# Two edits to the transfers of a fused attention and two-layer network kernel: the queue of the outputs, and the program place of the next phase's weight loads

## The chip, the cores and the metric

The kernel runs on one core of a Trainium2 chip. A core has five engines that run side by side, each through its own list of instructions in order: TensorE (PE: matrix products, with the weight loads in PEld), VectorE (DVE), ScalarE (ACT), GpSimd (POOL) and SyncE (SP), which here only issues transfers. A transfer (DMA) is issued by an instruction in an engine's list, waits there for its semaphores, and then runs on 16 DMA engines that all queues share. The metric is the device time of one execution in microseconds (us); the median of several runs counts. Before the change it is 1300.45 us (three runs: 1300.34, 1300.45, 1306.09).

## The reference

```python
def _attn_ref(q, k, v, tau):            # 4 batches, 8 heads, 576 rows, 64 wide
    scores = (1 / sqrt(64)) * q @ k.T
    scores = where(scores >= max(scores) - tau, scores, -1e9)
    attn = exp(scores - max(scores));  attn /= sum(attn) + 1e-9
    return attn @ v
x = attn_out as (2304, 512)              # 4 x 576 tokens
h = x @ w_in;  g = (a0 + a1*h + a2*h^2 + a3*h^3) / (1 + |b0|*|h| + |b1|*h^2 + 1e-6)
x = g @ w_out                            # w_in 512 x 2048, w_out 2048 x 512
h = x @ w2_in;  g = h if h >= 1, 0 if h <= -1, else (h + 1)^2 / 4
return g @ w2_out                        # (2304, 512) float32
```

## The kernel before

Each batch passes through three stages: attention, the first network (MoE1, `m == 0`) and the second (MoE2, `m == 1`). The networks run in eight phases, MoE1 and MoE2 of batch 0, then of batch 1, and so on (L664). A phase has 24 steps (L665): three blocks `j` of 192 tokens, and in each block the eight chunks `i` of the inner width of 2048. A step makes the first product (L645, into `ph`), a nonlinear function on ACT and DVE, a split into two float16 parts (`gg`, ACT L191 and POOL L195), and, three steps later (`LAG`), the second product (L659, into `acc`). Attention of batches 1 to 3 is cut into units that are laid beside the steps of the networks of the batch before (`ATTENTION`, L32): batch 1 beside steps 18 to 50, batch 2 beside 60 to 100, batch 3 beside 108 to 147.

The weights of one network, in float16 parts, fill eight tiles `wc` of 1 MB, one per chunk. Both networks share these eight places, so at each of the seven changes of phase the next phase's chunk `i` is loaded from scratch memory into the place of chunk `i` (`load_chunk`, L259) once the last block's second product has used it. L703 and L704 do this at the end of `finish_step`, in the last block, directly after that second product has been written into the program. The load waits for TensorE's last matmul on the place; that wait follows from the tile pool, whatever the place in the program.

At the end of a block of MoE2, `end_moe2` (L613) scales `acc` (ACT L615), turns it by TensorE (L621), copies each of two pieces out of PSUM by ACT (L623, tile `ot`) and issues a transfer of the piece to the output (L629): 24 transfers in all, of 128 or 256 KB.

All transfers are issued from SP's list: inputs (L310, L313), the transposes by DMA of attention's probabilities (L384, `eT` from `hl`, 144 of them, one per row block), those of q and k (L333), chunk loads (L261) and outputs (L629). An `eT` transpose waits for POOL's last piece of `hl` (L382) and is waited for by TensorE's product with v (L397). A later transfer in SP's list is not issued while an earlier one waits.

The order in each engine's list isn't written out by hand: the framework's scheduler sets it with a modelled time line, by readiness and by priorities given through `at(step)`, L158. Transfers take one of eight completion semaphores in turn, and one waits until the former transfer on its semaphore has landed.

Of the kernel before, what the change touches and what calls it, by code (L numbers as in the profile page):

```python
# [36 lines left out]
def tile_attention_moe_moe2(  # L37
# [18 lines left out]
    V, A, G, T, Q = nc.vector, nc.scalar, nc.gpsimd, nc.tensor, nc.sync  # L56
# [8 lines left out]
    NCH = 8  # L65
# [190 lines left out]
    def new_chunk(m, i):  # L256
        return wp.tile([P, 2 * HALF], F16, name=f"wc{m}_{i}", tag="wc")

    def load_chunk(m, i):  # L259
        wc = new_chunk(m, i)  # L260
        Q.dma_start(wc, scratch[m][i])  # L261
        return wc
# [334 lines left out]
    def flat(t):  # L597
        return t.rearrange("p (z d) t -> p z d t", z=2)
# [14 lines left out]
    def end_moe2(b, j, acc, consts):  # L613
        o = mp.tile([P, KT, TB], F32, name=f"o{b}_{j}", tag="yo", bufs=1)
        A.activation(flat(o), acc[:, :, 0 : 2 * TB].rearrange("p z (d t) -> p z d t", d=2), AF.Copy, scale=consts[4])  # L615
        cuts = sorted({j * TB, (j + 1) * TB} | {t * P for t in range(NT + 1) if j * TB < t * P < (j + 1) * TB})
        for c0, c1 in zip(cuts, cuts[1:]):
            n, t, p0 = c1 - c0, c0 // P, c0 % P
            pt = ps_1.tile([P, DM], F32, name=f"pt{b}_{j}_{c0}", tag="aux")
            for d in range(KT):  # L620
                T.transpose(pt[0:n, d * P : (d + 1) * P], o[:, d, c0 - j * TB : c1 - j * TB], ident)  # L621
            ot = mp.tile([P, DM], F32, name=f"ot{b}_{j}_{c0}", tag="wt", bufs=N_WT)
            A.copy(ot[0:n], pt[0:n])  # L623
            dst = out[b * S : (b + 1) * S, :]
            if t < NT:
                dst = dst[0 : NT * P, :].rearrange("(p t) d -> t p d", t=NT)[t, p0 : p0 + n, :]
            else:
                dst = dst[c0:c1, :]
            Q.dma_start(dst, ot[0:n])  # L629

    chunks = {}

# [20 lines left out]
    def second_product(m, i, gg, acc):  # L653
        w = chunks[m, i][:, HALF:].rearrange("p (x f d) -> p x f d", x=2, f=NF)
        for f in range(NF):
            for d in range(KT):
                dst = acc[:, d // 2, (d % 2) * TB : (d % 2 + 1) * TB]
                for n, (wx, gx) in enumerate(((0, 0), (0, 1), (1, 0))):
                    T.matmul(dst, w[:, wx, f, d * P : (d + 1) * P], gg[:, gx, f, :],  # L659
                             start=(i == 0 and f == 0 and n == 0 and d % 2 == 0),  # L660
                             stop=(i == NCH - 1 and f == NF - 1 and n == 2), skip_group_check=True)
# [9 lines left out]
    for n in range(N_UNITS):  # L671
        with at(2 * n - 40):
            next(att)
        while halves and len(halves) * N_UNITS > 2 * NCH * (N_UNITS - 1 - n):
            with at(2.4 * (2 * NCH - len(halves)) - 40):
                i, x = halves.pop(0)
# [11 lines left out]
        spread(first, last, [("att", b)] * N_UNITS)  # L688
    spread(*WEIGHTS, [("w", i, x) for i in range(NCH) for x in range(2)])

    pending, consts, accs, atts = [], {}, {}, {}

    def finish_step():
        n, m, b, j, i, gg, _ = pending.pop(0)
        if i == 0:
            accs[m, b, j] = ps_2.tile([P, 1024], F32, name=f"acc{m}_{b}_{j}", tag="acc").rearrange("p (z n) -> p z n", z=2)
        acc = accs[m, b, j]
        behind = pending[-1][-1] if n > 0 and len(pending) == LAG else None
        with tc.issue_after(behind) if behind is not None else nullcontext():
            second_product(m, i, gg, acc)  # L700
        if i == NCH - 1:
            (end_moe1 if m == 0 else end_moe2)(b, j, acc, consts[m, b, j])
        if j == NB - 1 and n + 1 < len(phases) and phases[n + 1][0] != m:  # L703
            chunks[1 - m, i] = load_chunk(1 - m, i)  # L704

    for st, (n, m, b, j, i) in enumerate(steps):
        with at(st):
            if i == 0:
                if m == 0:
                    consts[m, b, j] = moe1_consts(b) if j == 0 else consts[m, b, 0]  # L710
                else:
                    if b == 0 and j == 0:
                        moe2_weights()
                    consts[m, b, j] = moe2_consts(b, j)
            gg, last = first_product(m, b, j, i, consts[m, b, j])
        pending.append((n, m, b, j, i, gg, last))
        if len(pending) > LAG:
            with at(st + 1.5):
                finish_step()
        for t, u in beside[st]:  # L720
            if u[0] == "w":
                with at(t - 3):
                    stage_half(1, u[1], u[2], False)
            else:
                if u[1] not in atts:
                    atts[u[1]] = attention(u[1])
                with at(t - 1.5):
                    next(atts[u[1]])
    while pending:
        with at(st + 1.5):  # L730
            finish_step()
# [28 lines left out]
```

## Time and profile before

| | |
|---|---|
| median of three runs | 1300.45 us |
| profiled execution, device time | 1302.72 us |
| its span, first to last instruction | 1300.9 us |
| busy: PE, DVE, ACT, POOL | 1053.0, 1018.2, 841.7, 569.0 us |
| mean granted clock of TensorE | 0.925 of full speed |
| SP's transfers: packets' time on the 16 engines | 56.2% of the span |

A stretch of the span stands as start:end in us. In the rows, `SPq` is SP's issuing list, and `SPq L629 <- ACT ot L623` is time in which SP stood at a transfer of L629 until ACT had done L623. A duration of an issue is the time that SP spent issuing; the landing of the data comes later. `x2` merges two like instructions, with the time from the start of the first to the end of the last. Busy time of a stretch counts each engine apart, and a group's share over the whole run mixes stages with different limits, so the rows below are mostly of single stretches.

### The profile page before, as it was taken

Reading aid. Unit: us, or ns where it says so; the run is one execution under the profiler, and the core shown is the slowest. Engines: PE = TensorE matmul, PEld = TensorE weight load, DVE = VectorE, ACT = ScalarE, POOL = GpSimd, SP = SyncE. Lnnn points to the kernel's source line nnn. Section 1 sums busy time; section 2 is a strip of 40 time slices with the busy share of each in tenths; the row PEclk is TensorE's granted clock in tenths of the full one; section 3 lists DMA queues with packets and bytes.
Section 4 is the critical chain, followed back from the end, with each engine's and each line's share of the span. In section 5 each row is a group of like instructions: output and inputs, shape, how many; then the busy total and the mean of one; then the engine's idle time right before and its main releaser. Section 6 shows DMA issues by size and latency. Waiting matters only on the chain.

```text
span 1300.9 us, 31793 instructions
## 1 busy us (share of the span) xinstructions
PE 1053.0 (81%) x12498; PEld 959.5 (74%) x12498; DVE 1018.2 (78%) x2461; ACT 841.7 (65%) x1515; POOL 569.0 (44%) x781
## 2 busy tenths in 40 slices
PE   1465445687745888899889999999799999999998
PEld 1243324687744787789878898898688898999997
DVE  6667777899959887679999676889998677897431
ACT  4767655776745666667776576777765667776332
POOL 3858665454433545431146365422354554122221
PEclk9996656888966999999999999999989999999999
DMA  7878896323577667881279376911765669106100
GB/s 220 222 172 218 233 230 195 129 101 112 196 276 208 120 111 122 184 217 40 62 189 231 71 130 137 246 30 42 192 176 122 102 105 266 47 2 209 52 14 26
DMA packets 260277, 187.14 MB, mean 144 GB/s; under 512 B 220960, under 2 KB 233248, under 8 KB 251936
## 3 DMA queue, kind: packets, MB, share of 16 engines
q1 hardware_dynamic: 260128, 185.12, 56.2%
q8 instruction: 98, 1.61, 0.5%
q14 instruction: 51, 0.42, 0.1%
HBM read 106.96 MB, written 21.50 MB: 99 GB/s over the span
## 4 chain that ended last, share of the span: by engine, by line
PE 30%; DVE 26%; DMA 13%; issue 10%; POOL 10%; ACT 6%; SPq 2%; DVEq 0%; POOLq 0%; ACTq 0%
PE acc L659 13%; PE ph L645 13%; DMA eT<-hl 8%; POOL hl L382 5%; DVE e L371 2%; DMA qkT<-qk 2%; POOL wc L195 2%; PE pv L397 2%; DVE t L532 2%; DVE t L537 2%; DVE t L538 2%; DMA rqk<-in_k_dram 2%; DVE t L539 1%; DVE wt L212 1%; DVE sc L414 1%
## 5 line engine op out<-in xcount | busy, mean ns | idle before, releaser
L659 PE MATMUL acc<-gg,wc 128*128 128x192 f16 x4608 | 429.3, 247 | 11.0 <-POOL gg L195 4.6
L645 PEld LDWEIGHTS <-wc 128*128 128x128 f16 x4608 | 394.8, 100 | 48.1 <-DVE t L534 25.8
L659 PEld LDWEIGHTS <-wc 128*128 128x128 f16 x4608 | 384.0, 98 | 11.6 <-issue 10.2
L195 POOL TENSOR_TENSOR gg<-t,gg 128x384 f16<-128x384 f32 x192 | 190.5, 993 | 442.5 <-ACT gg L191 353.5
L645 PE MATMUL ph<-xT,wc 128*128 128x192 f16 x2304 | 220.8, 254 | 33.8 <-DVE t L534 32.9
L645 PE MATMUL ph<-yT,wc 128*128 128x192 f16 x2304 | 221.3, 250 | 1.8 <-DVE t L592 1.4
L382 POOL TENSOR_TENSOR hl<-e,hl 128x256 f16<-128x256 f32 x288 | 212.7, 759 | 0.0
L397 PE MATMUL pv<-v,eT 128*128 128x65 f16 (+1 forms) x2240 | 107.6, 207 | 75.3 <-DMA eT<-hl 74.8
L397 PEld LDWEIGHTS <-eT 128*128 128x128 f16 (+1 forms) x2240 | 94.4, 109 | 92.6 <-DMA eT<-hl 88.9
L191 ACT CAST gg<-t 128x384 f16<-128x384 f32 x192 | 97.0, 508 | 83.7 <-DVE t L592 35.1
L380 POOL TENSOR_TENSOR hl<-e,hl 128x64 f16<-128x64 f32 x144 | 53.5, 371 | 189.9 <-ACT hl L379 189.4
L379 ACT CAST hl<-e 128x576 f16<-128x576 f32 x144 | 95.9, 668 | 53.0 <-DVE e L371 40.0
L591 DVE SCALAR_TENSOR_TENSOR t<-t,c 128x384 f32<-128x384 f32 x96 | 64.8, 675 | 71.5 <-ACT t L590 71.2
L360 PE MATMUL s<-qkT 128*128 128x512 f16 (+2 forms) x320 | 93.3, 326 | 31.4 <-DVE e L371 13.1
L371 DVE SCALAR_TENSOR_TENSOR e<-sc,nt,e 128x576 f32<-128x576 f32 x108 | 95.1, 881 | 30.1 <-ACT e L370 29.6
L370 ACT ACTIVATE e<-sc,nt,con 128x576 f32<-128x576 f32 x108 | 93.5, 866 | 8.3 <-POOL hl L382 1.9
L590 ACT ACTIVATE t<-ph,c 128x384 f32<-128x384 f32 x96 | 63.9, 666 | 53.7 <-PE ph L645 48.8
L414 DVE TENSOR_SCALAR_CACHE_REDUCE sc<-s 128x576 f32<-128x576 f32 x108 | 80.9, 749 | 14.1 <-PE s L361 13.8
L415 ACT ACTIVATE nt<-mx,ln_e,con 128x1 f32<-128x1 f32 x144 | 55.1, 384 | 56.3 <-DVE sc L414 41.6
L530 ACT ACTIVATE t<-ph,sc 128x384 f32<-128x384 f32 x96 | 55.2, 576 | 56.1 <-PE ph L645 55.8
L535 ACT ACTIVATE t<-t,lc 128x384 f32<-128x384 f32 x96 | 67.8, 707 | 24.0 <-DVE t L532 23.6
L361 PE MATMUL s<-kT,qkT 128*128 128x512 f16 (+2 forms) x320 | 74.5, 324 | 2.0 <-DMA kT<-qkT 2.0
(172 smaller groups left out, 1649.2 us busy)
## 6 DMA issues: line engine op xcount, KB each, us to landing
wc<-scratch SPq DMA_DIRECT2D x56, 1024.0 KB, 5.7
rw<-in_moe_w_in_dram SPq DMA_DIRECT2D x16, 1024.0 KB, 5.7
rw<-in_moe_w_out_dram SPq DMA_DIRECT2D x16, 1024.0 KB, 5.9
scratch<-wc SPq DMA_DIRECT2D x8, 1024.0 KB, 6.0
scratch<-wh SPq DMA_DIRECT2D x16, 512.0 KB, 2.6
kT<-qkT SPq DMA_DIRECT2D x32, 144.0 KB, 2.5
rqk<-in_q_dram SPq DMA_DIRECT2D x16, 256.0 KB, 3.1
rqk<-in_k_dram SPq DMA_DIRECT2D x16, 256.0 KB, 3.2
```

Of the source, the lines that this page charges most:

```text
L191: A.copy(hi, src)
L195: G.tensor_tensor(lo[:, p], src[:, p], hi[:, p], op=ALU.subtract)
L360: T.matmul(s[rows, at : at + w], qkT[:, c, cols], k1[:, k0 : k0 + w], start=True, stop=False)
L361: T.matmul(s[rows, at : at + w], qkT[:, c, cols], k2[:, k0 : k0 + w], start=False, stop=True)
L370: A.activation(e, s, AF.Exp, bias=nb, scale=con[:, 0:1])
L371: V.scalar_tensor_tensor(e, s, th, e, op0=ALU.is_ge, op1=ALU.mult)
L379: A.copy(hi, e)
L382: G.tensor_tensor(lo_w[:, p], e[:, whole][:, p], hi[:, whole][:, p], op=ALU.subtract)
L397: T.matmul(pv[rows, 0:w], eT[:, c, cols], vv[:, h * NT + x if x < NT else H * NT + h, at : at + w], start=(n == 0), stop=(n == len(blocks) ...
L414: V.tensor_scalar(s, banks[:, 0:S], 1.0, -LARGEST, op0=ALU.mult, op1=ALU.max, accum_out=mx)
L645: last = T.matmul(ph[:, f, :], w[:, wx, kt, f * P : (f + 1) * P], rhs, start=(n == 0), stop=(n == 3 * KT - 1))
L659: T.matmul(dst, w[:, wx, f, d * P : (d + 1) * P], gg[:, gx, f, :], start=(i == 0 and f == 0 and n == 0 and d % 2 == 0), stop=(i == NCH - 1 ...
```

## The change

Two edits. Outputs are issued by ACT (`A`), not SP (`Q`). And the load of chunk `i` is written into the program after the second product of chunk `i + 2`, with that step's priority; after the last chunk, what is left in the list follows at once.

```diff
-            Q.dma_start(dst, ot[0:n])
+            A.dma_start(dst, ot[0:n])
...
-    pending, consts, accs, atts = [], {}, {}, {}
+    pending, consts, accs, atts, free = [], {}, {}, {}, []
...
         if j == NB - 1 and n + 1 < len(phases) and phases[n + 1][0] != m:
-            chunks[1 - m, i] = load_chunk(1 - m, i)
+            free.append((1 - m, i))
+        while free and (len(free) > 2 or i == NCH - 1):
+            c = free.pop(0)
+            chunks[c] = load_chunk(*c)
```

What it makes of SP's list at the change from MoE2 of batch 0 to MoE1 of batch 1, beside the end of attention of batch 1 (`eT1_2_2_2` is batch 1, head pair 2, unit 2, row 2; `wc0_1` is MoE1's chunk 1, `ot0_1_192` the output of batch 0 from token 192; the last number is the tile's own). SP before:

```order
L261 DMA wc0_0_6819<-scratch0_124 128x4096
L384 DMA_TRANSPOSE eT1_2_2_2_6720<-hl1_2_2_2_6715 128x9x128
L629 DMA out_0_dram<-ot0_1_192_6606 64x512
L384 DMA_TRANSPOSE eT1_3_0_0_6898<-hl1_3_0_0_6893 128x9x128
L261 DMA wc0_1_6877<-scratch0_124 128x4096
L629 DMA out_0_dram<-ot0_1_256_6614 128x512
L384 DMA_TRANSPOSE eT1_3_0_1_6934<-hl1_3_0_1_6929 128x9x128
L384 DMA_TRANSPOSE eT1_3_0_2_6978<-hl1_3_0_2_6973 128x9x128
L261 DMA wc0_2_7051<-scratch0_124 128x4096
L384 DMA_TRANSPOSE eT1_3_1_0_7130<-hl1_3_1_0_7125 128x9x128
L261 DMA wc0_3_7109<-scratch0_124 128x4096
```

And SP after, at the same place:

```order
L261 DMA wc0_0_7047<-scratch0_124 128x4096
L384 DMA_TRANSPOSE eT1_2_2_2_6720<-hl1_2_2_2_6715 128x9x128
L261 DMA wc0_1_7105<-scratch0_124 128x4096
L384 DMA_TRANSPOSE eT1_3_0_0_6894<-hl1_3_0_0_6889 128x9x128
L384 DMA_TRANSPOSE eT1_3_0_1_6930<-hl1_3_0_1_6925 128x9x128
L261 DMA wc0_2_7289<-scratch0_124 128x4096
L384 DMA_TRANSPOSE eT1_3_0_2_6974<-hl1_3_0_2_6969 128x9x128
L384 DMA_TRANSPOSE eT1_3_1_0_7126<-hl1_3_1_0_7121 128x9x128
L261 DMA wc0_3_7386<-scratch0_124 128x4096
```

The outputs are gone from SP. The loads stand where they stood, give or take one transpose: `wc0_1` and `wc0_2` each one transpose earlier. At the other six changes of phase the loads stand between the same transposes as before.

ACT's list at the same place (`e`, `nt`, `hl` are the softmax of batch 1, `t2` and `gg` MoE2's nonlinear function). Before:

```order
L379 CAST hl1_3_0_0_6893<-e1_3_0_0_6890 128x576
L415 ACTIVATE nt1_3_0_1_6921<-mx1_3_0_1_6920,ln_e_121,con1_3_5728 128x1
L623 COPY ot0_1_192_6606<-pt0_1_192_6601 64x512
L370 ACTIVATE e1_3_0_1_6926<-sc1_3_0_1_6922,nt1_3_0_1_6921,con1_3_5728 128x576
L590 ACTIVATE t21_0_2_5_7020<-ph1_0_2_5_6995,c20_2_6296 128x384
L379 CAST hl1_3_0_1_6929<-e1_3_0_1_6926 128x576
L623 COPY ot0_1_256_6614<-pt0_1_256_6609 128x512
```

And ACT after:

```order
L379 CAST hl1_3_0_0_6889<-e1_3_0_0_6886 128x576
L623 COPY ot0_1_192_6606<-pt0_1_192_6601 64x512
L629 DMA out_0_dram<-ot0_1_192_6606 64x512
L415 ACTIVATE nt1_3_0_1_6917<-mx1_3_0_1_6916,ln_e_121,con1_3_5728 128x1
L191 CAST gg1_0_2_5_7020<-t21_0_2_5_7016 128x384
L370 ACTIVATE e1_3_0_1_6922<-sc1_3_0_1_6918,nt1_3_0_1_6917,con1_3_5728 128x576
L623 COPY ot0_1_256_6614<-pt0_1_256_6609 128x512
L415 ACTIVATE nt1_3_0_2_6961<-mx1_3_0_2_6960,ln_e_121,con1_3_5728 128x1
L629 DMA out_0_dram<-ot0_1_256_6614 128x512
L379 CAST hl1_3_0_1_6925<-e1_3_0_1_6922 128x576
```

The issue of an output now stands in ACT's list right behind its copy, or one instruction later, and the softmax of the next row block is queued behind it.

A little earlier in SP's list (`rqk2_0`: q and k of batch 2, `qkT1_3` and `kT21_3`: q and k of batch 1's last head pair, transposed). SP before:

```order
L384 DMA_TRANSPOSE eT1_2_0_2_6211<-hl1_2_0_2_6206 128x9x128
L333 DMA_TRANSPOSE qkT1_3_5737<-qk1_3_5716 128x18x128
L310 DMA rqk2_0_8346<-in_q_dram 128x2x256
L384 DMA_TRANSPOSE eT1_2_1_0_6380<-hl1_2_1_0_6375 128x9x128
L335 DMA kT21_3_5739<-qkT1_3_5737 64x1152
L336 DMA kT21_3_5739<-qkT1_3_5737 64x1152
L384 DMA_TRANSPOSE eT1_2_1_1_6426<-hl1_2_1_1_6421 128x9x128
L313 DMA rqk2_0_8346<-in_q_dram 64x64 x2
L310 DMA rqk2_0_8346<-in_k_dram 128x2x256
L313 DMA rqk2_0_8346<-in_k_dram 64x64 x2
L384 DMA_TRANSPOSE eT1_2_1_2_6462<-hl1_2_1_2_6457 128x9x128
```

And after:

```order
L333 DMA_TRANSPOSE qkT1_3_5737<-qk1_3_5716 128x18x128
L384 DMA_TRANSPOSE eT1_2_0_2_6211<-hl1_2_0_2_6206 128x9x128
L335 DMA kT21_3_5739<-qkT1_3_5737 64x1152
L336 DMA kT21_3_5739<-qkT1_3_5737 64x1152
L310 DMA rqk2_0_8346<-in_q_dram 128x2x256
L384 DMA_TRANSPOSE eT1_2_1_0_6380<-hl1_2_1_0_6375 128x9x128
L313 DMA rqk2_0_8346<-in_q_dram 64x64
L384 DMA_TRANSPOSE eT1_2_1_1_6426<-hl1_2_1_1_6421 128x9x128
L313 DMA rqk2_0_8346<-in_q_dram 64x64
L310 DMA rqk2_0_8346<-in_k_dram 128x2x256
L384 DMA_TRANSPOSE eT1_2_1_2_6462<-hl1_2_1_2_6457 128x9x128
```

The five small loads of q and k that stood in one block ahead of `eT1_2_1_2` are now spread between the transposes, and `qkT1_3` stands ahead of `eT1_2_0_2`, not behind it. On TensorE, DVE and ACT the order of neighbouring instructions shifts by a few places from here to the start of MoE1 of batch 1, and in short pieces at two later changes of phase; no instruction is added or taken away but the moved issues.

## Rows read from the trace of the kernel before

**Rows 1.** Windows: stretch, length, busy PE, PEld, DVE, ACT, POOL; clock; DMA.
```profile
495.00:570.00 75.00, 67.77 (x871) 60.70 (x870) 52.40 (x145) 50.49 (x95) 37.91 (x63) 0.94 0.80 172
760.00:840.00 80.00, 76.72 (x1050) 70.51 (x1048) 57.70 (x153) 55.48 (x106) 41.63 (x68) 1.00 0.80 166
1015.00:1100.00 85.00, 82.41 (x1131) 76.15 (x1132) 60.67 (x154) 58.39 (x111) 45.42 (x71) 1.00 0.71 157
1100.00:1283.00 183.00, 181.18 (x2197) 180.39 (x2195) 116.61 (x251) 99.90 (x179) 41.39 (x46) 1.00 0.21 69
```
**Rows 2.** PE's waits in 495:570, 760:840, 1015:1100: total us, times, longest.
```profile
PE pv L397 <- DMA eT<-hl: 7.2, 5, 2.4
...
PE pv L397 <- DMA eT<-hl: 3.2, 5, 1.0
...
PE pv L397 <- DMA eT<-hl: 2.9, 5, 1.4
```
**Rows 3.** SP's waits: two of the whole run, then 1130:1301, then 495:570.
```profile
SPq L261 <- PE acc L659: 142.9, 36, 61.1
SPq L629 <- ACT ot L623: 128.2, 15, 35.4
...
SPq L629 <- ACT ot L623: 90.1, 6, 35.4
...
SPq L261 <- PE acc L659: 6.3, 3, 2.7
```
**Rows 4.** Timeline of SP, 530:563: start, duration, instruction, count.
```profile
540.55 0.42 SPq L629 DMA_DIRECT2D out_dram<-ot  x1
541.06 6.17 SPq L384 DMA_TRANSPOSE eT<-hl  x2
548.48 0.33 SPq L261 DMA_DIRECT2D wc<-scratch  x1
...
554.41 0.33 SPq L261 DMA_DIRECT2D wc<-scratch  x1
```
**Rows 5.** Timeline of POOL, 512:542: the last pieces of two `hl` tiles.
```profile
518.42 1.30 POOL L382 TENSOR_TENSOR hl<-e,hl 128x256 f16<-128x256 f32 x2
...
539.36 1.29 POOL L382 TENSOR_TENSOR hl<-e,hl 128x256 f16<-128x256 f32 x2
```
**Rows 6.** Timeline of SP, 512:525.
```profile
520.76 1.11 SPq L313 DMA_DIRECT2D rqk<-in_k_dram  x2
522.03 3.71 SPq L384 DMA_TRANSPOSE eT<-hl  x2
```
**Rows 7.** Issue durations ns min/median/max: L629 whole run, L384 in 495:570.
```profile
L629 SPq DMA_DIRECT2D out_dram<-ot x24: 337/479/742, 497.1 to 1297.4; - x24
...
L384 SPq DMA_TRANSPOSE eT<-hl x17: 1242/1804/2619, 499.4 to 564.6; - x17
```
**Rows 8.** Timeline of ACT, 586:589.5.
```profile
587.08 0.58 ACT L623 COPY ot<-pt 128x512 f32<-128x512 f32 x1
587.56 0.70 ACT L535 ACTIVATE t<-t,lc 128x384 f32<-128x384 f32 x1
588.30 0.61 ACT L536 ACTIVATE t<-t,lc 128x384 f32<-128x384 f32 x1
```
**Rows 9.** Timeline of the last instructions, all engines, 1290:1301.
```profile
1295.46 0.58 ACT L623 COPY ot<-pt 128x512 f32<-128x512 f32 x1 [0.75 <-PE pt L621]
1296.07 1.81 SPq L629 DMA_DIRECT2D out_dram<-ot  x2
...
1296.81 0.58 ACT L623 COPY ot<-pt 64x512 f32<-64x512 f32 x1 [0.76 <-PE pt L621]
```
**Rows 10.** The profile's transfers: the chunk load, KB each, us to landing.
```profile
wc<-scratch SPq DMA_DIRECT2D x56, 1024.0 KB, 5.7
```
**Rows 11.** Timeline of PE, 545:566: MoE1's first two first products.
```profile
554.22 0.91 PE L645 MATMUL ph<-xT,wc 128*128 128x192 f16 x9
557.88 0.82 PE L645 MATMUL ph<-xT,wc 128*128 128x192 f16 x8
```

## The prediction

> **What bounds the kernel now.** I read the windows first, since the busy shares of the whole run mix stages. The edits act in three kinds of stretch: the ends of MoE2 phases, where outputs and chunk loads meet attention of the next batch (495:570, 760:840, 1015:1100), the starts of MoE1 phases, where the last two outputs of a batch leave, and the last phase. In the three stretches PE is busy 67.77 of 75, 76.72 of 80 and 82.41 of 85 us; it is idle 7.2, 3.3 and 2.6 us, 13.1 in all [rows 1]. That is nearly all that a better order of transfers could give back there. In 1100:1283 PE is busy 181.18 of 183 us and ACT 99.90 [rows 1]: TensorE sets the time, and ACT has room. Then PE's waits: in the three stretches it stands 7.2, 3.2 and 2.9 us for a transposed `eT` at L397, five times in each [rows 2]. So the thing to follow is whether a transpose (L384) is late, and through what.
>
> Then SP's own waits. They look large: 128.2 us at output transfers until ACT had made the copy, and 142.9 us at chunk loads until TensorE was off the place [rows 3]. But 90.1 of the 128.2 us lie in the last 171 us, where no transpose is left to be held up [rows 3]. And elsewhere a wait of SP costs only if a transpose stands behind it with its input ready. The timelines of SP and POOL, laid side by side, tell this. The worst case behind an output: L629 is issued at 540.55 for 0.42 us, the transpose behind it starts at 541.06, and POOL's last piece for it had ended at 539.36 + 1.29 = 540.65; the transpose is 0.41 us late [rows 4, 5]. I went through the other transposes right behind an output in the same way: none had been ready before the output was issued. Behind chunk loads the picture is the same, with less than 1 us at the worst. SP stands there, but the row of `hl` that the next transpose needs isn't done yet. So neither kind of wait, as the trace of before has it, holds up much.
>
> **Outputs leave SP.** SP loses 24 issues of 479 ns at the median [rows 7], 11.5 us of its time. Of its waits only the 0.41 us above stood before a ready transpose. How much of a late transpose reaches the end: in 495:570 there are 17 transposes [rows 7] and PE had to wait for five [rows 2], so about 0.3 of the lateness passes. That gives 0.41 x 0.3 = 0.1 us gained.
>
> **Outputs enter ACT.** Each issue now occupies ACT's list. The trace has no issue from ACT; the nearest row is the issue of the same transfer from SP, 337 to 742 ns, 479 at the median [rows 7]. I take the median. It must also wait for ACT's own copy just before it. What that costs is seen at 587: L535, which does not read the copy, starts 0.10 us before the copy's end (587.56 against 587.08 + 0.58), while L536, which reads what L535 wrote, starts 0.04 us after its end (588.30 against 587.56 + 0.70) [rows 8]. The overlap lost is 0.14 us, so one output holds ACT 0.48 + 0.14 = 0.62 us, and 24 hold it 14.9 us. Six belong to the last phase, hidden under TensorE. Six leave in the starts of MoE1, with no transpose behind them. Twelve leave beside attention, 12 x 0.62 = 7.4 us; queued behind them are the softmax's casts (`hl`, L379), which POOL's pieces, the transposes and PE wait for. ACT is busy 50.49 of 75, 55.48 of 80 and 58.39 of 85 us there [rows 1], so about a third of its time is slack, and the next instructions often wait for DVE. I take the same share of 0.3 that passes for a late transpose: 2.2 us lost. The ends are 0 (all in slack) and 7.4 us.
>
> The eight semaphores add waits too. In the changed program an output on ACT waits for a transfer that was issued eight transfers before it in the program, and those had long landed when ACT made the copies; I take 0.
>
> **The last output.** The first of the final two copies ends at 1295.46 + 0.58 = 1296.04 and the second starts at 1296.81 [rows 9]. The issue of the first, 0.62 us, fits into that gap of 0.77 us, and SP had issued at 1296.07, just as soon as ACT could. So 0; if the issue takes 742 ns, 0.1 us is lost.
>
> **The loads two steps later.** This part barely moves anything in the built program. At six of the seven changes of phase the loads stand between the same transposes as before, and they wait for the same last matmuls; at the change near 530 two of them stand one transpose earlier, not later. The scheduler places a load where its model says the place comes free, and the later line in the program doesn't decide that. So it gives nothing by itself.
>
> **Places that shift at 500:570.** Two effects with opposite signs. The small loads of `rqk2_0` stood in a block before `eT1_2_1_2`: the block ended at 520.76 + 1.11 = 521.87, the transpose started at 522.03, and POOL had been done at 518.42 + 1.30 = 519.72, so it was 2.3 us late [rows 5, 6]. In the new order two of these loads, not five, stand between it and the transpose before it. On the other side four transposes (`eT1_3_0_0`, `eT1_3_0_2`, `eT1_3_1_2`, `eT1_3_2_1`) now stand behind a chunk load that stood after them. A load holds SP for its own wait on PE, up to 2.7 us here [rows 3]; four times that is 10.8 us. With 0.3 passing, the bounds are a gain of 0.7 and a loss of 3.2 us. The products that free the places also move ahead in PE's list, so that the loads' waits should shrink; the nearest row, the lateness of transposes behind loads before, is under 1 us, and I take 0.
>
> **Sum.** -0.1 + 2.2 + 0 + 0 + 0 = +2.1 us against the profiled execution's 1302.72 us (its span of 1300.9 and 1.8 around it), or 1304.8 us. That execution was 2.3 us slower than the median of the runs, 1300.45, so against the median I expect 1300.45 + 2.1 = 1302.5 us. A change of under 0.5% (6.5 us) is about what a measurement of this kernel can't tell from none.
>
> **Rivals.**
> *SP's list was the hidden limit (faster).* If the transposes of the first stretch come without PE waiting, its idle 7.2 us go: 1300.45 - 7.2 = 1293.3 us. For it: PE's waits there are on transposes [rows 2]. Against it: the transposes behind outputs and loads were ready late, not issued late.
> *ACT's issues are on the path (slower).* All of the 7.4 us passes: 1300.45 + 7.4 - 0.1 = 1307.8 us. Its place is ACT's list in the three stretches, between copy and next cast; it decides over the forecast once more than 0.8 of each hold reaches a transpose that PE waits for. For it: the cast of the next row stands right behind an issue in the new order. Against it: ACT's slack of a third.
> *ACT's issue must wait while SP issues (slower).* A transpose occupies SP for 1.8 us at the median in 495:570 [rows 7], and 17 of them fill about 0.4 of the stretch. If an issue from ACT can't run beside one from SP, each of the twelve can take up to 1.8 us more, 21.6 us at the utmost; with all of it on the path the time is 1307.8 + 21.6 = 1329 us, with 0.3 of it passing 1302.5 + 6.5 = 1309 us. No row of before has two engines issuing, so this stays open. The Trainium skill has a rule for it: "Perfetto Trace Analysis", section "DMA Instruction — HWDGE (DVE, Sync)", says that the block which makes the descriptors is locked for one instruction at a time, and that the wait for that lock counts in the recorded duration of the issue. By that rule, a lengthening of ACT's issues would be seen in their own rows.
> *The loads do come two loads later (slower).* If chunk 1 were loaded when chunk 3 was, at 554.41, it would land 5.7 us later at 560.1 [rows 4, 10], 2.2 us after PE first used it at 557.88 [rows 11]; chunk 0, at 548.48, would land just at its first use at 554.22. Over seven changes that is 15.6 us, 1318 us. Against it stands the built order of SP.
>
> **How the numbers follow.** Forecast 0.54. SP as hidden limit 0.20. ACT's issues on the path 0.16. Waits for SP's issue 0.07. Later loads 0.03. The first rival is the only case of faster: 0.20. The forecast's own range, with ACT's ends of 0 and 7.4 and the shifted places' -0.7 and +3.2, is 1300 to 1309; its upper end alone passes 0.5%, so I give it to "same". The slower cases together are 0.26, but ACT's issues at 1307.8 lie just beyond the bound of 1307, so I move 0.02 of them to "same": faster 0.20, same 0.56, slower 0.24. The range is drawn from 1294, which leaves out the full gain, to 1310, which leaves out later loads and full waiting for SP.
>
> **What would show it.** SP's waits at L629 gone, and PE's waits for `eT` in the three stretches still near 13 us: the first step right. ACT's rows at L629 of about 0.5 us with the next cast 0.6 us later, and idle time of POOL before `hl` up by a few us: the second; issues of 2 us there: the third rival. Chunk loads that start within some tenths of a us after TensorE's last use of the place: the loads haven't moved. I am wrong if PE's idle time in 495:570 falls by more than half, or if 760:840 and 1015:1100 grow by more than 3 us each.

## The result, and the profile after

The changed kernel takes 1308.55 us (median of 22 runs, 1302.24 to 1317.62), the kernel before 1302.47 us (22 runs beside it, 1297.79 to 1308.26). The ratio is 1.0051, 95% interval 1.0035 to 1.0067: 6.1 us or half a per cent slower, which is little, but 1 lies outside the interval. The forecast was 1302.5 us with 1294 to 1310. The two profiled executions took 1311.15 and 1302.72 us, 8.4 us apart, so the rows show somewhat more than the median loss; and a window is a stretch of time, which in the slower kernel holds a little less of the program.

The windows of the profile after, to be laid beside [rows 1] (stretch, length, busy PE, PEld, DVE, ACT, POOL; clock; DMA share, GB/s):

```profile
495.00:570.00 75.00, 65.08 (x842) 57.79 (x839) 52.56 (x139) 47.39 (x91) 35.02 (x57) 0.95 0.79 166
760.00:840.00 80.00, 73.68 (x1011) 67.43 (x1007) 56.27 (x148) 55.20 (x104) 43.81 (x69) 1.00 0.74 154
1015.00:1100.00 85.00, 81.01 (x1099) 74.40 (x1097) 58.57 (x151) 56.52 (x107) 46.34 (x72) 1.00 0.70 137
1100.00:1283.00 183.00, 181.06 (x2214) 180.29 (x2212) 121.79 (x261) 104.02 (x189) 44.09 (x50) 1.00 0.24 79
```

PE's idle time in the three stretches with attention beside them is 9.9, 6.3 and 4.0 us where it was 7.2, 3.3 and 2.6: 7.1 us more, most of the 8.2 us between the two spans (1309.1 and 1300.9 us). In the last stretch PE is as full as before. So the loss lies in the main where attention runs beside the ends of MoE2. PE's waits of the profile after in 495:570, 760:840 and 1015:1100 answer to [rows 2] (total us, times, longest):

```profile
PE pv L397 <- DMA eT<-hl: 9.8, 5, 2.9
...
PE pv L397 <- DMA eT<-hl: 4.0, 5, 2.0
...
PE pv L397 <- DMA eT<-hl: 4.0, 5, 1.1
```

They add up to 17.8 us, against 13.3. PE waits more for the same thing as before, a transposed `eT`. SP's own waits, the first two of the whole run and the third of 495:570, answer to [rows 3]:

```profile
SPq L261 <- PE acc L659: 150.3, 35, 71.7
...
SPq L759 <- DMA out_dram<-ot: 90.2, 2, 57.2
...
SPq L261 <- PE acc L659: 4.2, 5, 2.3
```

The waits at L629 are gone; what SP waits for at L759 is only the end of the program. The outputs in ACT's list (issue duration ns min/median/max, and us from issue to landing) answer to [rows 7]:

```profile
L629 ACTq DMA_DIRECT2D out_dram<-ot x24: 333/426/524, 497.6 to 1305.9; - x24
...
DMA to landing us min/median/max: 2.0/2.4/6.5
```

An issue from ACT is no longer than one from SP was (426 against 479 ns at the median). ACT around one of them, and at the program's end [rows 9] (start us, duration us, instruction, idle before it and its releaser):

```profile
541.40 0.56 ACT L623 COPY ot<-pt 128x512 f32<-128x512 f32 x1
541.87 0.39 ACT L415 ACTIVATE nt<-mx,ln_e,con 128x1 f32<-128x1 f32 x1
542.00 0.35 ACTq L629 DMA_DIRECT2D out_dram<-ot  x1
542.44 0.67 ACT L379 CAST hl<-e 128x576 f16<-128x576 f32 x1 [0.19 <-DVE e L371]
...
1303.96 0.58 ACT L623 COPY ot<-pt 128x512 f32<-128x512 f32 x1 [0.75 <-PE pt L621]
1304.57 0.34 ACTq L629 DMA_DIRECT2D out_dram<-ot  x1
...
1305.26 0.58 ACT L623 COPY ot<-pt 64x512 f32<-64x512 f32 x1 [0.72 <-PE pt L621]
```

Here the issue begins 0.04 us after the copy's end, beside another instruction, and the cast behind it starts 0.09 us after the issue's end, with 0.19 us of idle time before it. The last lines show the first of the final two issues inside a gap in which ACT waits for PE anyway. What is new in the profile's list of queues (packets, MB, share of 16 DMA engines) is the second line; before there was one queue for all of this:

```profile
q1 hardware_dynamic: 257440, 180.40, 54.4%
q10 hardware_dynamic: 2688, 4.72, 1.2%
```

### The profile page after: what moved, and what is told of

It reads as the page before. It is cut to its first block, busy times and chain, and to the rows that moved or that the text cites. A ratio compares the mean times of both kernels' runs of the same rounds, so it can differ in the third digit from the quotient of the medians.

```text
span 1309.1 us, 31793 instructions
## 1 busy us (share of the span) xinstructions
PE 1050.7 (80%) x12498; PEld 958.0 (73%) x12498; DVE 1021.6 (78%) x2461; ACT 840.1 (64%) x1515; POOL 570.6 (44%) x781
## 4 chain that ended last, share of the span: by engine, by line
PE 31%; DVE 26%; DMA 15%; issue 9%; POOL 8%; ACT 6%; SPq 2%; ACTq 0%; DVEq 0%; POOLq 0%
PE ph L645 13%; PE acc L659 13%; DMA eT<-hl 11%; POOL hl L382 4%; DVE e L371 3%; PE pv L397 2%; POOL wc L195 2%; DVE t L537 2%; DVE t L532 2%; DVE t L538 2%; DMA qkT<-qk 2%; DVE sc L414 1%; DVE t L539 1%; DVE wt L212 1%; DVE wt L213 1%
## 5 line engine op out<-in xcount | busy, mean ns | idle before, releaser
L382 POOL TENSOR_TENSOR hl<-e,hl 128x256 f16<-128x256 f32 x288 | 209.5, 747 | 0.0
L380 POOL TENSOR_TENSOR hl<-e,hl 128x64 f16<-128x64 f32 x144 | 57.1, 396 | 192.4 <-ACT hl L379 190.7
L414 DVE TENSOR_SCALAR_CACHE_REDUCE sc<-s 128x576 f32<-128x576 f32 x108 | 80.7, 748 | 14.9 <-PE s L361 14.7
```

Of the source, the lines that this page charges most:

```text
L382: G.tensor_tensor(lo_w[:, p], e[:, whole][:, p], hi[:, whole][:, p], op=ALU.subtract)
L414: V.tensor_scalar(s, banks[:, 0:S], 1.0, -LARGEST, op0=ALU.mult, op1=ALU.max, accum_out=mx)
```

## The experiments

The program's lists are made by a scheduler, and moving the outputs changes more than the engine of 24 instructions: the order of PE, POOL, ACT and SP differs too. So most kernels here are built twice. The first build gives the lists of the kernel before (or of the changed one); in the second, these lists are laid down as the order of every engine, and only the edit differs. "Old order" and "new order" below mean that. All kernels were timed in turns with the kernel before.

**Engine or order?** The four corners are the kernel before, the changed kernel and these two.

```
act_old_order:  (Q -> A).dma_start(dst, ot[0:n])   each right behind its copy; all other lists: old order
sp_new_order:   Q.dma_start(dst, ot[0:n])          all other lists: new order
```

> The 24 outputs are issued from ScalarE, each right behind its copy; every other instruction of every engine stands in the order of the kernel before. Theory A (the loss of about 6 us comes from ScalarE's own issues, about 0.4 us each, and from outputs on a second ring beside the transposes): slower by 4 to 6 us, ratio 1.003 to 1.005. Theory B (the loss comes from the other order that the scheduler makes of the lists once the outputs have left SyncE, chunk loads in front of transposes above all): within 2 us of before, ratio 0.999 to 1.0015, and PE's busy time in 495:570 near before's 67.8 us, not after's 65.1. By the prediction's own term (0.3 of the hold passes, 2.2 us) it would be 1.0017.

> The outputs stay on SyncE; every other instruction of every engine stands in the order of the changed kernel. Theory A (ScalarE's issues cost): ratio 0.999 to 1.0015. Theory B (the order costs): slower by 4 to 6 us, ratio 1.003 to 1.005, with the late starts of steps after the first and second change from MoE2 to MoE1, as in the changed kernel, and PE busy near 65 us in 495:570. If both share the loss, both kernels lie near 1.002 to 1.003.

| | old order | new order |
|---|---|---|
| outputs from SP | 1 (before) | 1.0021 (1.0000 to 1.0042) |
| outputs from ACT | 1.0070 (1.0046 to 1.0095) | 1.0051 (1.0035 to 1.0067) |

Outputs from ACT in the old order lose 9 us (1309.38 against 1299.95), all of the loss and more. The new order on its own loses 2.7 us, with an interval that reaches to zero. So the issuing engine is the cause, whatever it is that the engine brings with it, and the order at most a small part; the two do not add up, and the intervals don't say whether the new order makes the outputs on ACT any better. ACT in the kernel before, then in the kernel with outputs from ACT in the old order, at the same copy:

```profile
535.85 0.56 ACT L623 COPY ot<-pt 64x512 f32<-64x512 f32 x1
536.31 0.87 ACT L370 ACTIVATE e<-sc,nt,con 128x576 f32<-128x576 f32 x1
```

```profile
532.85 0.56 ACT L625 COPY ot<-pt 64x512 f32<-64x512 f32 x1
533.44 0.48 ACTq L631 DMA_DIRECT2D out_dram<-ot  x1
533.96 0.87 ACT L372 ACTIVATE e<-sc,nt,con 128x576 f32<-128x576 f32 x1 [0.56 <-POOL hl L384]
```

In before the instruction behind this copy starts 0.10 us ahead of the copy's end; here it starts 0.55 us behind it. That is a hold of 0.65 us, where the prediction had 0.62. (The profile puts the idle time down to POOL, whose piece ended at 533.88; the issue ended last, at 533.92.) Behind 17 of the 24 copies the next instruction starts within 0.1 us of the issue's end, 0.40 to 0.62 us behind the copy; behind six it starts later still, and the last has none behind it. The obvious reading is that this hold is the price. It is wrong.

**The second edit alone, and the second edit as its words have it.**

```
loads_edit_alone:  outputs from Q; the list `free` as in the change
loads_two_later:   outputs from Q; in SP's list the load of chunk i stands where that of chunk i+2 stood
```

> Only the second edit (the list of free places), outputs on SyncE. The order of every engine is that of the kernel before, so every theory that puts the cause into order or engine gives a ratio of 1.000, 0.999 to 1.001. If the edit does something that the order does not show: beyond 1.002 or below 0.998.

> The kernel before, outputs on SyncE, but each of the eight chunk loads at a change of phase stands in SyncE's list where the load two later stood (the last three together). This is the second edit as its words have it. If loads that come two later are late for TensorE, as the rival of the prediction had it: 15.6 us slower, ratio 1.012. If the transposes that now stand ahead of the loads gain what the loads lose: ratio 0.998 to 1.002, with PE's waits for the transposed eT below the 13 us of before in the three stretches and its waits for wc above before's.

The edit alone gives 1.0003 (0.9989 to 1.0018): nothing, as the lists said, which it leaves as they were. Its trace is a second execution of the program before, and shows what chance does: single steps begin up to 4.9 us apart in the two. Loads that do come two later give 1.0114 (1.0090 to 1.0138), 14.7 us. PE's waits in that kernel, 480:1100:

```profile
PE pv L399 <- DMA eT<-hl: 17.5, 18, 2.6
PE ph L648 <- DMA wc<-scratch: 15.5, 7, 3.9
```

PE now waits for chunks, 15.5 us in seven waits; it waits less for `eT`, 17.5 us against 24.3 and 24.9 in the two executions of the program before, since transposes stand ahead of loads. The loss is larger than the difference of the two.

**ACT's occupied list or the second queue?** Four kernels, all in the old order.

```
hold_alone:            Q.dma_start(dst, ot[0:n]);  + 3 one-element copies on ACT behind each output copy
hold_twice:            the same with 6 copies
act_beside_attention:  A.dma_start for the 12 outputs beside attention, Q.dma_start for the other 12
act_in_slack:          A.dma_start for all 24, each up to 23 ACT instructions behind its copy,
                       ahead of an instruction before which ACT waited anyway
```

> Outputs on SyncE and every list as in the kernel before; behind each of the 24 output copies ScalarE does three extra one-element copies (the first reads the output tile, each next one the one before it; their result goes nowhere). With copies of so small a size at 0.20 us each, the instruction behind starts about 0.62 us after the output copy ends, against 0.4 to 0.6 us where the output was issued there. Theory H (the loss is ScalarE's occupied list): slower by 4 to 10 us, ratio 1.003 to 1.0075, near the 1.007 that outputs on ScalarE cost in the same order. Theory R (the loss is the second ring: output transfers that run beside the transposes' instead of in line with them): 0.999 to 1.0015.

> As the kernel with the extra copies on ScalarE, but six of them behind each output copy instead of three (about 1.4 us instead of 0.7 of occupied list). Theory H: about twice that kernel's loss, ratio 1.007 to 1.015. Theory R: 0.999 to 1.003.

> Every list as in the kernel before; only the 12 outputs that leave beside attention are issued from ScalarE behind their copies, the other 12 stay on SyncE. Both theories put the loss beside attention: ratio 1.004 to 1.009, that of all 24 on ScalarE (1.007). If the starts of the MoE1 phases or the last phase have the loss: 0.999 to 1.002.

> All 24 outputs are issued from ScalarE, every other instruction stands in the order of the kernel before, but an issue stands up to 23 ScalarE instructions behind its copy, ahead of one before which ScalarE waited 0.4 to 1.9 us in the trace of before. Theory H: nothing is lost, 0.998 to 1.0015. Theory R: still 1.004 to 1.009, since the ring and the bytes on it are the same.

| kernel | ratio | 95% interval |
|---|---|---|
| hold_alone | 1.0007 | 0.9988 to 1.0027 |
| hold_twice | 1.0053 | 1.0034 to 1.0072 |
| act_beside_attention | 1.0057 | 1.0033 to 1.0080 |
| act_in_slack | 1.0056 | 1.0033 to 1.0078 |

The first and the last row decide. ACT around the same copy in hold_alone, then in act_in_slack:

```profile
535.63 0.56 ACT L625 COPY ot<-pt 64x512 f32<-64x512 f32 x1
536.23 0.19 ACT L634 COPY hold<-ot 64x1 f32<-64x1 f32 x1
536.45 0.41 ACT L635 COPY hold<-hold 64x1 f32<-64x1 f32 x2
536.77 0.86 ACT L372 ACTIVATE e<-sc,nt,con 128x576 f32<-128x576 f32 x1
```

```profile
532.04 0.56 ACT L625 COPY ot<-pt 64x512 f32<-64x512 f32 x1
532.51 0.87 ACT L372 ACTIVATE e<-sc,nt,con 128x576 f32<-128x576 f32 x1
...
535.95 0.87 ACT L372 ACTIVATE e<-sc,nt,con 128x576 f32<-128x576 f32 x1
536.20 0.47 ACTq L631 DMA_DIRECT2D out_dram<-ot  x1
536.72 0.50 ACT L193 CAST gg<-t 128x384 f16<-128x384 f32 x1
```

In the first, ACT's next instruction starts 0.58 us behind the copy (536.77 against 536.19), the hold of an output on ACT without the output, and the kernel loses nothing that can be measured. In the second the next instruction starts 0.09 us ahead of the copy's end, the issue lies under another instruction, and the cast behind it isn't late: the output without the hold, and the loss is there. So the loss is with the transfers. The 12 that leave beside attention carry most of it at least (1.0057 of 1.0070, with intervals that overlap). A hold of twice the length does lose (1306.49 against 1300.48 us). ACT's slack hides 0.7 us a time, and not 1.3. One trace suggests another way for that loss: in hold_twice's waits in 480:1100, below, DVE waits 38.0 us for `e`, against 32.1 in hold_alone, while PE's waits for `eT` aren't longer.

```profile
DVE e L373 <- ACT e L372: 38.0, 35, 3.2
...
PE pv L399 <- DMA eT<-hl: 24.5, 27, 3.1
```

**The bytes or the queue?** Old order again; 12 outputs are cut to one row of 2 KB (the rest is left out), from ACT and from SP.

```
act_one_row:   A.dma_start(dst[0:1], ot[0:1])   for the 12 beside attention; the other 12 whole, from A
sync_one_row:  Q.dma_start(dst[0:1], ot[0:1])   for the 12 beside attention; the other 12 whole, from Q
```

> All 24 outputs are issued from ScalarE behind their copies, every other instruction in the order of the kernel before, but each of the 12 that leave beside attention writes one row of 2 KB only (its other 63 or 127 rows are left out). Theory R1 (the output's bytes take turns with the transposes in flight, which land later): the loss goes with the bytes, ratio 0.998 to 1.002. Theory R2 (a transfer on the second ring costs whatever its size, by its issue or by the switch between rings): still 1.004 to 1.009.

> Outputs on SyncE, all in the order of the kernel before; the same 12 outputs write one row of 2 KB only (the rest is left out). It shows what the bytes cost where they stand in line with the transposes. Theory R1: in line they stand behind the transposes issued before them and cost little, ratio 0.997 to 1.000, and the kernel with one row from ScalarE lies within 0.002 of this one. Rival of the prediction (SyncE's list is a hidden limit through the outputs): 0.994 to 0.996 would show that the outputs in line hold up transposes after all.

1.0005 (0.9988 to 1.0022) and 0.9998 (0.9980 to 1.0016). Without their bytes outputs on ACT cost nothing that can be measured, so neither the issue nor the second queue as such has a price. And the same bytes in SP's line cost nothing either: leaving them out gains nothing. Only bytes on the second queue cost. (The cut takes packets along with the bytes: by the profile's list of queues one of these outputs makes 2 packets on ACT's queue where a whole one makes 112 on average. The two weren't tried apart. A one-row issue is also shorter, 0.23 us; hold_alone and act_in_slack say that this isn't the reason. PE's waits for `eT` in act_one_row's one execution, 27.0 us, are no lower than those of act_beside_attention, 27.4: a single trace settles less than the timed runs.)

What the bytes do there is read from PE's waits and from the landings. First PE's waits for `eT` in 480:1100 of the kernel before (24.9 us in loads_edit_alone, 25.5 in hold_alone, both with outputs on SP):

```profile
PE pv L397 <- DMA eT<-hl: 24.3, 26, 2.4
```

The same of the changed kernel:

```profile
PE pv L397 <- DMA eT<-hl: 31.4, 25, 2.9
```

The same of act_old_order:

```profile
PE pv L399 <- DMA eT<-hl: 28.6, 25, 3.4
```

The same of act_in_slack:

```profile
PE pv L399 <- DMA eT<-hl: 28.8, 26, 2.8
```

In these three PE waits 3 to 7 us longer for the same transposes. The waits alone don't settle it, since sp_new_order, with outputs on SP, has this:

```profile
PE pv L399 <- DMA eT<-hl: 28.2, 24, 3.2
```

The times of the transposes in the traces tell the two apart. Added up over the last 96 of the 144 transposes, the times from issue to landing are 414, 409, 411 and 398 us where outputs are on SP (before, loads_edit_alone, hold_alone, hold_twice), and 425, 426, 423 and 419 us where all 24 or, in the last, 12 are on ACT (changed, act_old_order, act_in_slack, act_beside_attention). sp_new_order has 413, and with the 12 cut to one row it is 414 from ACT and 409 from SP: the transposes land later only where whole outputs leave by the second queue. The new order shows at another place, in the delay from POOL's last piece of `hl` to the transpose's issue. Over the same 96 it adds up to 26 to 27 us in before, loads_edit_alone and hold_alone and to 27 to 29 in the three old-order kernels with whole outputs on ACT, but to 34 in sp_new_order and 32 in the changed kernel.

In the packet records of the trace, 800 to 1,600 of the transposes' 256-byte packets started between an output's own first and last packet, summed over the 12 outputs, with outputs on SP (before, loads_edit_alone, hold_alone, hold_twice, sp_new_order, sync_behind_two), and 2,900 to 3,600 in the four kernels with whole outputs on ACT. So on two queues the transposes' packets and the outputs' ran mixed, and each kind took longer: the 12 outputs of act_old_order need 52 us in sum to land, against 47 in before, so they weren't faster for having a queue of their own. The step from these landings to the time rests on single executions: the waits in these traces grow by 3 to 7 us where the timed loss is 6 to 9, and act_beside_attention was profiled in its quickest execution (1300.43 us, median 1307.16).

The Trainium skill ("DMA: Bandwidth & Descriptors", section "Queues, rings and completion order") says that each DMA engine takes turns between the queues that have work, packet by packet; within a queue it takes up its work in order. The traces agree, by the two counts of packets above: in line, an output waits its turn behind the transposes that were issued before it; on its own queue it takes turns with them, and PE waits for some of them. How the turns are shared out no run here shows. The Trainium skill's "Perfetto Trace Analysis", section "DMA Optimizations", says that it may make sense, above all with loops or control flow, to give inputs to one engine and outputs to another. Here that costs 0.5 to 0.7%, and the measurement decides.

**Two tries at a faster kernel.**

```
sync_behind_two:  outputs from Q, each of the 12 behind the next two transposes of SP's list
loads_one_later:  outputs from Q; at the five changes of phase with attention, the loads of
                  chunks 0 to 3 stand one load's place later
```

> Outputs on SyncE and whole; in SyncE's list each of the 12 that leave beside attention stands behind the next two transposes. If transposes right behind an output in line are held up by its bytes: 0.996 to 0.999, a kernel that beats both. If the outputs in line cost nothing: 0.999 to 1.001. If a held output keeps the next copy from its buffer: above 1.002.

> Outputs on SyncE, lists of the kernel before, but at the five changes of phase that have attention beside them the first four of eight chunk loads stand one load's place later in SyncE's list; the other four stay. In the two executions of the program of before these loads landed 8.6 to 17.5 us ahead of their first use and stand 2 to 11 us apart. If transposes that no longer stand behind a load land sooner and no load comes late: part of the 6.8 us that PE's waits for eT fell by when all eight came two later, 2 to 4 us gained, ratio 0.997 to 0.9985, which beats both kernels. If the loads then crowd before the fifth, or the transposes ahead gain nothing: 0.999 to 1.002. If PE waits for wc again: above 1.003.

Both are slower: 1.0041 (1.0021 to 1.0061) and 1.0052 (1.0034 to 1.0071). In loads_one_later PE waits for no chunk; every load landed at least 4.5 us ahead of its first use at the five changes. But chunks 3 and 4 are then issued 0.7 to 2 us apart, and single transposes behind such a pair land after 9.6 and 9.8 us (8.4 at most from 480 us on in the two executions of the program before). Its PE waits in 480:1100:

```profile
PE pv L399 <- DMA eT<-hl: 26.1, 21, 4.2
```

The longest wait is 4.2 us where it was 2.6, the sum is hardly up, and the profiled execution was a quick one, so this shows where a loss arises and not all 6.8 us of it. Why sync_behind_two loses isn't settled: its one trace has no longer waits for `eT` (23.3 us), and before the program's end no engine in it waits for an output to land, which a buffer that is held too long would show. No version here beats the kernel before.

## Why the prediction was right, and where it was not

The time fell into the range, near its upper end, and the kernel became slower, as forecast. That the range holds it is luck: the sum consists of ACT's hold, which costs next to nothing, and what the loss comes from stood in no term. The ratio of 1.0051 lies on the bound of 0.5% between "no change", held likeliest, and "slower", with its interval across it. The size was off: 2.1 us forecast, 6.1 measured (9 with outputs on ACT in the old order). The forecast time also starts from 1300.45 us, where the kernel before took 1302.47 beside the changed one.

- **Outputs leave SP: -0.1 us.** Right. sync_one_row shows that the 12 outputs beside attention cost nothing measurable in SP's line, so nothing could be gained. This also refutes the first rival, SP's list as the hidden limit: the waits of 128.2 us at L629 [rows 3] went, and PE waited more, not less. The prediction's sign for this step, PE's waits still near 13 us, failed all the same (17.8), through the next point.
- **Outputs enter ACT: +2.2 us.** This is the step that failed. The hold itself was well sized (0.62 forecast, 0.65 in the row above), but its price is that of hold_alone, 0.9 us with an interval from -1.6 to 3.5 (the ratio's, times 1300.5): most of it is slack. The loss of 6 to 9 us comes from something for which the prediction had no term: the outputs' bytes, on a queue of their own, take turns with transposes. I had treated a transfer that changes its queue as the same transfer and had priced the issue alone. The idle time of POOL before `hl`, which should have grown by a few us, didn't (126.8 us against 130.3 in 480:1100): the trace after spoke against ACT's list before any experiment did.
- **The rival "ACT's issues are on the path", 1307.8 us,** came nearest in number, with the wrong mechanism: its hold is there, and does not matter.
- **Waits for lanes, the last output: 0.** Right; no issue was longer than 0.53 us, and the last ones lie in gaps.
- **ACT's issue waits for SP's.** Not seen. In the changed kernel six issues of transposes on SP overlapped with an issue from ACT, in act_old_order eight, and ACT's issues took 333 to 524 ns in the one and 333 to 529 in the other. Of the six, four ran wholly inside an issue of SP that took 1.3 to 2.0 us, and they took 334 to 350 ns (128 rows) and 488 ns (64 rows), where all of the changed kernel's took 333 to 378 and 473 to 524. The rule of a lock that the prediction takes from the Trainium skill ("Perfetto Trace Analysis", section "DMA Instruction — HWDGE (DVE, Sync)") doesn't show here as a longer issue.
- **The loads two later: 0.** Right: 1.0003. (At the change near 530 us SP's timeline after shows four loads earlier, not two: chunks 1, 2 and 5 by one transpose, chunk 4 by two.) The rival that they really come later was priced at 15.6 us; loads_two_later costs 14.7, with PE's waits for chunks of 15.5 us in seven waits. That the sums agree is partly luck, since waits for `eT` fell by 7 us, which the price had left out.
- **Places that shift: 0, with -0.7 to +3.2.** sp_new_order has 2.7 us (0 to 5.5): the bounds hold to their upper part, and 0 was too low, if the order costs at all. Neither effect came as it was priced. The small loads that are spread out gain nothing: `eT1_2_1_2` is issued 2.3 us late in the changed kernel as before, and the three transposes ahead of it 3.5, 2.8 and 2.5 us late, where only one of them had been over 1 us late (1.6). The transposes behind chunk loads of this change are late by at most 0.5 us, not 2.7.

## What to carry to other kernels

A transfer that moves to another engine's queue leaves its place in line. If small transfers that something waits for run at that time, price its bytes and not only its issue; a queue with long waits at its head is no sign that leaving it helps. To separate an edit from what a scheduler makes of it, fix the order of every list and change one thing; and to tell an occupied engine from its side effects, put a dummy of equal length in its place, and the real thing where the engine idles.

## What the runs showed of the hardware that was not expected

4.7 MB of outputs, 1.2% of the DMA engines' time, cost 6 to 9 us on a second queue; of these the 12 outputs beside attention, 2.4 MB, alone have a ratio of 1.0057 there, and in SP's line they cost nothing that can be measured (0.9998 without their bytes). The last 96 transposes took 398 to 414 us in sum to land with the outputs in line or cut to one row (loads_two_later, with its loads elsewhere, 385), and 419 to 426 with whole outputs on the second queue. The issue of a transfer from ACT took 0.33 to 0.53 us whether or not SP was issuing, and the one with fewer rows took longer: 333 to 378 ns for 128 rows, 473 to 524 for 64 in the changed kernel. ACT hid 0.6 to 0.7 us of hold, 24 times, without a measurable loss, but not 1.3.
